# One-time weight sums moved from VectorE to GpSimd, and a ring tile for the fourth difference, in a fused attention and feed-forward kernel

## The chip, the cores and the metric

The kernel runs on one core of a Trainium2 chip. The core has five engines, each with an instruction queue of its own that is worked off in order: TensorE (matrix products; PE in the profile, with PEld for its weight loads), VectorE (DVE), ScalarE (ACT), GpSimd (POOL) and SyncE (SP, which here only issues DMA transfers). GpSimd's queue issues DMA transfers too. Engines wait for one another through semaphores. Data lie in on-chip memory (SBUF), matrix products end in accumulator banks (PSUM), and some intermediate sums are kept in DRAM.

The metric is the time of one execution in device microseconds. The median of three runs before the change is 679.04 us.

## What is computed

Linear attention with a decay for each head, over 4 batches, 8 heads, 768 positions and 64 channels, whose output is the input of a feed-forward block:

```python
for b in range(nb):                     # blocks of 64 positions
    intra = np.einsum('bhic,bhjc->bhij', qb, kb) * Dmask[None]
    intra = np.einsum('bhij,bhjd->bhid', intra, vb)
    inter = np.einsum('bhid,bhde->bhie', qb * lam_pow[None], kv_state)
    out[:, :, sl] = intra + inter
    kb_dec = kb * rev_pow[None]
    kv_state = lam_block[None, :, None, None] * kv_state + np.einsum('bhsd,bhse->bhde', kb_dec, vb)
...
x = attn_out.transpose(0, 2, 1, 3).reshape(B * S, H * D)   # 3072 tokens, 512 channels
h = x @ w_in                                               # 512 x 2048
g = h - np.tanh(h)
return (g @ w_out).astype(np.float32)                      # 2048 x 512
```

All arithmetic is in 32-bit floats.

## The kernel before

The 768 positions are worked in six groups of 128 (`g` is 0 to 5), each with all four batches: 512 tokens. For a group the attention makes `xt`, `up` multiplies with `w_in` in four steps `u`, ScalarE and VectorE apply `h - tanh(h)` and leave the hidden tiles `g11`, `g12`, `g21`, `g22` and `gS1`, and `down` multiplies with `w_out`. From the second group on, a product of two 2x2 block matrices is not made of eight block products but of seven, numbered 1 to 7, by Winograd's form of Strassen's scheme; `FACT` names the two factors of each. The factors are sums and differences of quarters:

- of `w_in` in `sums_in` (L250, four VectorE operations of 128x512 for each `u`: S1, S2, S3 in place, S4),
- of `w_out` in `sums_out` (L256 to L259), kept in DRAM as `factors`,
- of the hidden tiles in `sums_once` (L672) and `seeded_sums`.

Several of the seven products are split by the same scheme once more. Their small factors are made once and serve all later groups:

- `inner_weights(u, ns)` (L531) makes, from the quarters of a factor of `w_in`, four sums of 128x128 (L538) into a tile `ws2` and stores three of them in DRAM as `fine_in` (L539). It is called in the second group (`g` = 1) for factors 2 and 4, then 1, then 5.
- `factors_twice(t)` (L631) does that for a factor of `w_out`: `load_quarters(t)` fetches four quarters from `factors` (L628, tiles `wq` for the first set and `oq` from the pool `opool` after it), then four differences of 128x512 (L636) are made and each is stored in `fine` (L637). `MADE` gives the factor of each of the five sets: 5, 6, 4, 7, 3. The first two sets are made in the second group, one difference in a step; the other three in the third group, two in a step. The table `TURNS` gives the steps.

The tiles `ws2`, `wt1`, `wt2`, `wt4`, the sums `s1` and `s2` of `sums_twice` (L725, L726) and the token sums `tt2` (L548) share one ring of four slots of 128x512, the tag "sums". Whoever takes a slot waits until its former tile is read for good, by a transfer to DRAM too.

`down_twice(g, n, zw)` works a product that is split again: seven groups of four small products (L741), in the order 1, 2, 6, 5, 7, 3, 4. Group 6 needs `s2` (L726), group 3 needs the sum of L746. Its pieces of `fine` come through `piece` (L640), as do those of `factors` and `fine_in`: a ring of eight tiles `wb`, all loaded from GpSimd's queue (L647, L650, L653). Using a piece sends the loads of later ones, up to seven ahead; a load waits until TensorE is done with its slot's former piece. `seeded` does the second product of the hidden layer for `g` from 2 on, `inner_steps` (L566) the products with small factors of `w_in`.

The attention of the group after next is worked between these products (`run(p0[...])`, `run(p1[...])`); in it, `att_state` multiplies keys by their decay on VectorE (L350) before TensorE's kv products (L363).

`hidden(g, c)` is the hidden tile `c` of group `g`. There is one buffer for each `c`, which all groups use in turn. Tile 22 of the third group (`GI` is 2) is first written by the products with factor 5 of `w_in`; in the second group the last to read tile 22 is product 4 of `down`.

Instructions are put in order by a list scheduler at build time; `tc.keep_in_program_order` ties some of them to the program's order.

Of the kernel before, what the change touches and what calls it, by code (L numbers as in the profile page):

```python
# [9 lines left out]
F32 = mybir.dt.float32  # L10
# [6 lines left out]
AL = mybir.AluOpType  # L17
# [7 lines left out]
def kernel(  # L25
# [32 lines left out]
    nc = tc.nc  # L58
# [8 lines left out]
    NU = DFF // 512  # L67
# [55 lines left out]
    raw, late = {}, {}  # L123
# [61 lines left out]
    GI = 2  # L185
# [56 lines left out]
        wt = wst.tile([128, 8, 256], F32, name="wt", tag="w")  # L242
        return wt[:, 0:4], wt[:, 4:8]

    def sums_in(u):
        a11, a12, a21, a22 = (w1[u][:, 2 * c:2 * c + 2, r] for r, c in ((0, 0), (0, 1), (1, 0), (1, 1)))
        s1, s2, s4 = (ws[u][:, x] for x in range(3))
        for dst, x, y, op in ((s1, a21, a22, AL.add), (s2, s1, a11, AL.subtract), (a21, a11, a21, AL.subtract),
                              (s4, a12, s2, AL.subtract)):
            tc.keep_in_program_order(nc.vector.tensor_tensor(dst, x, y, op=op))  # L250

    def sums_out(kt):
        bt, tt = pair[kt]
# [178 lines left out]
    def hidden(g, c):  # L432

        if (g, c) not in hid:
            hid[g, c] = gpool.tile([128, NU, 2, HB], F32, name=f"g{c}", tag=f"g{c}")
        return hid[g, c]
# [85 lines left out]
    def seeded_sums(g, u):  # L522
        g11, g12, g22, s1 = (hidden(g, c)[:, u] for c in (11, 12, 22, "S1"))
        nc.vector.tensor_tensor(s1, g12, g22, op=AL.add)
        nc.vector.tensor_tensor(g12, g11, g12, op=AL.subtract)

    def a_quarter(n, u, i, k):
        wt = {1: w1[u][:, 0:2, 0], 2: w1[u][:, 2:4, 0], 4: w1[u][:, 2:4, 1], 5: ws[u][:, 0]}[n]
        return wt[:, k, ts(i, 128)]

    def inner_weights(u, ns):  # L531
        for n in ns:
            a11, a12, a21, a22 = (a_quarter(n, u, i, k) for i in range(2) for k in range(2))
            t = late["pool"].tile([128, 4, 128], F32, name="ws2", tag="sums", bufs=4)
            s1, s2, s4 = (t[:, x] for x in range(3))
            for dst, x, y, op in ((s1, a21, a22, AL.add), (s2, s1, a11, AL.subtract), (a21, a11, a21, AL.subtract),
                                  (s4, a12, s2, AL.subtract)):
                tc.keep_in_program_order(nc.vector.tensor_tensor(dst, x, y, op=op))  # L538
            nc.gpsimd.dma_start(out=fine_in[INNER.index(n)].rearrange("x p u c -> p u x c")[:, u], in_=t[:, 0:3])  # L539

    def inner_tokens(g, ns):
# [78 lines left out]
    def load_quarters(t):  # L620

        for i in range(2):
            for j in range(2):
                if t == 0:
                    x = late["pool"].tile([128, NU, 128], F32, name="wq", tag="wb", bufs=RING)
                else:
                    x = opool.tile([128, NU, 128], F32, name="oq", tag="o")
                nc.gpsimd.dma_start(out=x, in_=quarter_source(t, i, j))  # L628
                quarters[t, i, j] = x

    def factors_twice(t):  # L631

        b11, b12, b21, b22 = (quarters.pop((t, i, j)) for i in range(2) for j in range(2))
        t1, t2, t4 = (late["pool"].tile([128, NU, 128], F32, name=f"wt{x}", tag="sums", bufs=4) for x in (1, 2, 4))
        for x, dst, a, b in ((5, t1, b12, b11), (6, t2, b22, t1), (7, b12, b22, b12), (4, t4, b21, t2)):
            tc.keep_in_program_order(nc.vector.tensor_tensor(dst, a, b, op=AL.subtract))  # L636
            nc.gpsimd.dma_start(out=fine[TWICE.index(MADE[t]), SUB.index(x)], in_=dst)  # L637
            yield

# [128 lines left out]
    def every(steps):  # L768
        for _ in steps:
            pass  # L770
# [80 lines left out]
    def run(pieces):  # L851
        for fn, *args in pieces:
            fn(*args)
# [38 lines left out]
    for u, c, n, more in turns:  # L892
        every(up_plain(u, (c,)))
        weights(ready["done"] + n)
        run(more)
        if (u, c) == (1, 21):
            load(B + 2)
        if c == 22:
            sums_first(u)
            if u == 1:  # L900
                load_weights(NU * KI)
                load(2 * B)
                powers()
            if u == 2:
                sums_in(0)
# [4 lines left out]
    for kt in range(KH):  # L910
        down_first(kt, (1, 2))
        if kt + 1 < KH:
            sums_out(kt + 1)
        sums_late(kt)
        down_first(kt, (5, 4, 7, 6, 3) if kt + 1 < KH else (5, 6, 7, 4, 3))
        if kt + 3 < KH:
            weights(ready["done"] + 2)
        if kt == 2:
            sums_in(1)
# [4 lines left out]


    TURNS = {1: {t + x: n for n, t in ((0, 7), (1, 14)) for x in range(4)},
             2: {t + x // 2: n for n, t in ((2, 3), (3, 7), (4, 11)) for x in range(4)}}
    making = {}

    def make_factors(g, step):  # L930
        t = TURNS.get(g, {}).get(step)
        if t is not None:
            if t not in making:
                making[t] = factors_twice(t)
            for _ in range(g):
                next(making[t])
            if g == 2 and t < 4 and step in (4, 8):
                load_quarters(t + 1)
# [5 lines left out]
    for g in range(1, NG):  # L944
        last = g == NG - 1
        (p0, p1), step = ahead, 0
        for u in range(NU):
            if g < GI:
                for n in (2, 6, 5, 7, 1, 4, 3):
                    if n != 1:  # L950
                        up(g, u, n)
                    elif u + 1 < NU:
                        up(g, u + 1, 1)
                    else:
                        every(down(g, 1))
                    if u < 2 and n == 5:
                        sums_in(u + 2)
                    step += 1
                    make_factors(g, step)
                inner_weights(u, (2, 4))  # L960
                if u > 1:
                    run(p0[u - 2:u - 1])
                continue
            if u == 0:
                first = down(g, 1)
                if g == 2:
                    load_quarters(2)
            for n in (1, 7) if u == 0 else (6, 3, 1, 7) if u + 1 < NU else (7, 3, 1):
                if n == 1:
                    next(first)  # L970
                else:
                    seeded(g, u + (n == 6), n)
                if n == (7 if u + 1 < NU else 3):
                    seeded_sums(g, u)
                step += 1
                make_factors(g, step)
# [8 lines left out]
        if g < GI:  # L985
            for u in (0, 1):
                inner_weights(u, (1,))
# [4 lines left out]
        if g < GI:  # L992
            for u in (2, 3):
                inner_weights(u, (1,))
# [74 lines left out]
```

## Time and profile before

| what | value |
|---|---|
| median of three runs (lowest, highest) | 679.04 us (677.19, 680.48) |
| the profiled execution | 678.29 us, its span 676.5 us |
| mean granted TensorE clock | 0.992 |
| VectorE busy, share of the span | 490.4 us, 72% |
| GpSimd busy (nearly all of it DMA issues) | 229.2 us, 34% |
| loads of ring pieces from `fine`, L650 | 147, each 540 ns on GpSimd's queue |
| loads of ring pieces from `factors` and `fine_in`, L653 and L647 | 56 and 48 |
| mean rate of DRAM traffic | 201 GB/s |

The profile shows one execution. "Busy" of an engine excludes its waits, and DMA issues of GpSimd count as busy. In the lists of waits a line names the waiting engine, what it would write and its line, then what ended the wait. The table of stretches gives for each stretch of the span its length and the busy time of TensorE, its weight loads, VectorE, ScalarE and GpSimd (instructions in brackets), then the granted clock of TensorE, the DMA engines' busy share and their rate. A timeline line has the start and the length in microseconds, engine, line, operation and tiles, and in square brackets how long the engine had been idle before it and what ended that.

### The profile page before, as it was taken

How to read it: one execution, taken by the hardware profiler on the slowest of the kernel's cores; microseconds unless marked ns; L12 is line 12 of the kernel's file. 1: busy time of each engine (PE TensorE's matmuls, PEld its weight loads, DVE VectorE, ACT ScalarE, POOL GpSimd, SP SyncE). 2: the span in 40 equal slices, each digit the busy share in tenths (PEclk: the TensorE clock that was granted, in tenths of full speed). 3: DMA queues.
4: the chain of work that ended last, by engine and by line, in shares of the span. 5: the costliest groups of instructions: out<-in, count | busy, mean ns of one | idle time of the engine just before them, and what ended most of it. 6: DMA issues, size and time to landing. Idle time of an engine off the chain costs nothing.

```text
span 676.5 us, 13691 instructions
## 1 busy us (share of the span) xinstructions
PE 656.5 (97%) x5112; PEld 601.4 (89%) x5112; DVE 490.4 (72%) x923; ACT 218.4 (32%) x418; POOL 229.2 (34%) x397
## 2 busy tenths in 40 slices
PE   8998999999999899999699999999999999999998
PEld 6787888888888799987599998899998899998897
DVE  4577795737879576677888667998666988557963
ACT  4796825403321112422112233211243211243210
POOL 0001435745422444225444320144420154420261
PEclk9999999999999899999899999999999999999999
DMA  9989888968856778577898876298966176741294
GB/s 212 232 215 268 269 285 248 314 184 229 242 115 154 217 190 252 147 190 232 264 248 233 246 176 128 84 258 232 284 145 139 63 226 207 254 125 48 79 301 152
DMA packets 165475, 136.74 MB, mean 202 GB/s; under 512 B 134688, under 2 KB 135840, under 8 KB 165408
## 3 DMA queue, kind: packets, MB, share of 16 engines
q0 software_dynamic: 31728, 104.36, 48.1%
q1 hardware_dynamic: 133536, 31.50, 23.7%
q8 instruction: 41, 0.67, 0.4%
q14 instruction: 26, 0.21, 0.1%
q10 hardware_dynamic: 144, 0.00, 0.0%
HBM read 109.84 MB, written 25.95 MB: 201 GB/s over the span
## 4 chain that ended last, share of the span: by engine, by line
PE 81%; DMA 6%; DVE 4%; issue 3%; SPq 2%; ACT 1%; POOL 1%; DVEq 0%; POOLq 0%; ACTq 0%
PE y L741 11%; PE zw L741 8%; PE y L566 8%; PE plain L688 8%; PE acc L825 7%; PE y L509 6%; PE h L796 5%; PE y L447 4%; PE z L566 4%; PE zs L509 3%; PE sp L341 3%; PE op L395 2%; PE w L566 2%; DMA raw<-in_moe_w_in_dram 2%; PE z L447 2%
## 5 line engine op out<-in xcount | busy, mean ns | idle before, releaser
L650 POOL DMA_DIRECT2D wb<-fine x147 | 79.2, 540 | 172.0 <-PE plain L688 99.0
L688 PE MATMUL plain<-wb,g 128*128 128x256 f32 x352 | 81.5, 380 | 1.5 <-DVE g L493 1.5
L688 PEld LDWEIGHTS plain<-wb,g 128*128 128x128 f32 x352 | 65.9, 190 | 11.0 <-DVE g L493 2.3
L744 ACT ACTIVATE q<-y 128x128 f32<-128x128 f32 x84 | 23.3, 277 | 142.4 <-PE y L741 140.2
L796 PE MATMUL h<-xt,w 128*128 128x256 f32 x256 | 58.0, 383 | 3.9 <-DVE w L285 3.9
L796 PEld LDWEIGHTS h<-xt,w 128*128 128x128 f32 x256 | 47.7, 190 | 11.7 <-DVE w L285 3.9
L653 POOL DMA_DIRECT2D wb<-factors x56 | 30.2, 541 | 65.0 <-PE y L566 24.0
L741 PE MATMUL y<-wb,g 128*128 128x128 f32 x384 | 51.1, 278 | 0.0
L492 ACT ACTIVATE th<-g 128x512 f32<-128x512 f32 x48 | 29.4, 628 | 63.8 <-DVE g L518 63.8
L570 ACT ACTIVATE g<-y 128x512 f32<-128x512 f32 x48 | 28.5, 593 | 61.1 <-PE y L566 61.1
L741 PEld LDWEIGHTS y<-wb,g 128*128 128x128 f32 x384 | 46.4, 192 | 1.3 <-issue 0.5
L647 POOL DMA_DIRECT2D wb<-fine_in x48 | 25.9, 542 | 41.2 <-PE y L566 17.3
L206 POOL DMA_DIRECT2D raw<-in_moe_w_out_dram x16 | 8.7, 546 | 84.8 <-ACT r L282 59.1
L345 DVE TENSOR_TENSOR ss<-sp,mask 128x512 f32<-128x512 f32 x48 | 30.6, 682 | 9.0 <-PE sp L341 9.0
L741 PE MATMUL zw<-wb,g 128*128 128x128 f32 x256 | 34.8, 279 | 0.0
L493 DVE TENSOR_TENSOR g<-g,th 128x512 f32<-128x512 f32 x48 | 31.6, 685 | 2.7 <-ACT th L492 2.7
L825 PE MATMUL acc<-wt,g 128*128 128x256 f32 x144 | 32.9, 380 | 0.0
L741 PEld LDWEIGHTS zw<-wb,g 128*128 128x128 f32 x256 | 31.8, 195 | 0.1
L825 PEld LDWEIGHTS acc<-wt,g 128*128 128x128 f32 x144 | 27.2, 190 | 4.1 <-DVE g L832 0.4
L509 PE MATMUL zs<-xt,ws 128*128 128x256 f32 x128 | 30.6, 381 | 0.0
L509 PE MATMUL y<-tt,ws 128*128 128x256 f32 x128 | 30.4, 380 | 0.1
L509 PE MATMUL y<-xt,w 128*128 128x256 f32 x128 | 29.7, 379 | 0.0
(214 smaller groups left out, 1483.6 us busy)
## 6 DMA issues: line engine op xcount, KB each, us to landing
wb<-fine POOLq DMA_DIRECT2D x147, 256.0 KB, 4.0
wb<-factors POOLq DMA_DIRECT2D x56, 256.0 KB, 4.1
wb<-fine_in POOLq DMA_DIRECT2D x48, 256.0 KB, 4.2
raw<-in_moe_w_out_dram POOLq DMA_DIRECT2D x16, 512.0 KB, 6.0
v_nat<-in_v_dram SPq DMA_DIRECT2D x24, 256.0 KB, 5.5
fine<-wt POOLq DMA_DIRECT2D x24, 256.0 KB, 4.6
k_nat<-in_k_dram SPq DMA_DIRECT2D x20, 256.0 KB, 4.9
raw<-in_moe_w_in_dram SPq DMA_DIRECT2D x8, 512.0 KB, 6.0
```

Of the source, the lines that this page charges most:

```text
L345: tied(g == 0, nc.vector.tensor_tensor(ss[:, j], sp[j], mask[:, j], op=AL.mult))
L447: nc.tensor.matmul(out=t[:, m, :], lhsT=wt[:, kt, ts(m, 128)], rhs=x[:, kt, :], start=first and m == 0 and kt == 0, stop=kt == 1, skip_gro ...
L492: nc.scalar.activation(th, src, AF.Tanh)
L493: nc.vector.tensor_tensor(dst(c), src, th, op=AL.subtract)
L509: nc.tensor.matmul(out=t[:, m, :], lhsT=wt[:, kt, ts(m, 128)], rhs=x[:, kt, :], start=False, stop=kt == 1, skip_group_check=True)
L566: nc.tensor.matmul(out=dst[:, ts(u, 128)], lhsT=a, rhs=b, start=x in (1, 2, 5) and u == 0, stop=True, skip_group_check=True)
L650: nc.gpsimd.dma_start(out=t.rearrange("p m c -> p (m c)"), in_=fine[TWICE.index(n_), SUB.index(x_)].rearrange("p u c -> p (u c)"))
L653: nc.gpsimd.dma_start(out=t, in_=factors[XAT[FACT[n_][1]]][:, 2 * x_:2 * x_ + 2, :])
L688: nc.tensor.matmul(out=t[:, m, :], lhsT=a[:, u, kt, ts(m, 128)], rhs=wb[:, kt, :], start=first and u == 0 and m == 0 and kt == 0, stop=u = ...
L741: nc.tensor.matmul(out=dst, lhsT=a[:, u, :], rhs=wb[:, ts(u, 128)], start=x in (1, 2) and u == 0, stop=u == NU - 1, skip_group_check=True)
L796: tied(u == 0, nc.tensor.matmul(out=hm[c][:, m, :], lhsT=w1[u][:, i, a, ts(m, 128)], rhs=xt[0, t][:, i, :], start=m == 0 and i == 0, stop= ...
L825: nc.tensor.matmul(out=acc[n][:, r, :], lhsT=a[:, ts(r, 128)], rhs=b, start=kt == 0 and r == 0, stop=kt == KH - 1, skip_group_check=True)
```

## The change

Four edits:

- `sums_in` gets the engine as an argument; for `u` = 2 and 3 its four sums run on GpSimd instead of VectorE.
- `inner_weights` for factors 1 and 5 runs its four sums on GpSimd, and puts them into the buffer of hidden tile 22 of the third group instead of a slot of the ring "sums".
- `factors_twice` no longer writes the third difference over the loaded quarter `b12`, but into a tile `wt3` of its own from the ring. For the fourth and fifth set its differences run on GpSimd.
- In `TURNS` the fifth set starts at step 12 of the third group instead of 11.

```diff
-    def sums_in(u):
+    def sums_in(u, eng=nc.vector):
         a11, a12, a21, a22 = (w1[u][:, 2 * c:2 * c + 2, r] for r, c in ((0, 0), (0, 1), (1, 0), (1, 1)))
         s1, s2, s4 = (ws[u][:, x] for x in range(3))
         for dst, x, y, op in ((s1, a21, a22, AL.add), (s2, s1, a11, AL.subtract), (a21, a11, a21, AL.subtract),
                               (s4, a12, s2, AL.subtract)):
-            tc.keep_in_program_order(nc.vector.tensor_tensor(dst, x, y, op=op))
+            tc.keep_in_program_order(eng.tensor_tensor(dst, x, y, op=op))
...
     def inner_weights(u, ns):
         for n in ns:
             a11, a12, a21, a22 = (a_quarter(n, u, i, k) for i in range(2) for k in range(2))
-            t = late["pool"].tile([128, 4, 128], F32, name="ws2", tag="sums", bufs=4)
+            eng = nc.gpsimd if n in (1, 5) else nc.vector
+            if n in (1, 5):
+                t = hidden(GI, 22)[:, u].rearrange("p m (x c) -> p (m x) c", x=2)
+            else:
+                t = late["pool"].tile([128, 4, 128], F32, name="ws2", tag="sums", bufs=4)
             s1, s2, s4 = (t[:, x] for x in range(3))
             for dst, x, y, op in ((s1, a21, a22, AL.add), (s2, s1, a11, AL.subtract), (a21, a11, a21, AL.subtract),
                                   (s4, a12, s2, AL.subtract)):
-                tc.keep_in_program_order(nc.vector.tensor_tensor(dst, x, y, op=op))
+                tc.keep_in_program_order(eng.tensor_tensor(dst, x, y, op=op))
...
     def factors_twice(t):
 
         b11, b12, b21, b22 = (quarters.pop((t, i, j)) for i in range(2) for j in range(2))
-        t1, t2, t4 = (late["pool"].tile([128, NU, 128], F32, name=f"wt{x}", tag="sums", bufs=4) for x in (1, 2, 4))
-        for x, dst, a, b in ((5, t1, b12, b11), (6, t2, b22, t1), (7, b12, b22, b12), (4, t4, b21, t2)):
-            tc.keep_in_program_order(nc.vector.tensor_tensor(dst, a, b, op=AL.subtract))
+        t1, t2, t3, t4 = (late["pool"].tile([128, NU, 128], F32, name=f"wt{x}", tag="sums", bufs=4)
+                          for x in (1, 2, 3, 4))
+        eng = nc.gpsimd if t > 2 else nc.vector
+        for x, dst, a, b in ((5, t1, b12, b11), (6, t2, b22, t1), (7, t3, b22, b12), (4, t4, b21, t2)):
+            tc.keep_in_program_order(eng.tensor_tensor(dst, a, b, op=AL.subtract))
             nc.gpsimd.dma_start(out=fine[TWICE.index(MADE[t]), SUB.index(x)], in_=dst)
             yield
...
-             2: {t + x // 2: n for n, t in ((2, 3), (3, 7), (4, 11)) for x in range(4)}}
+             2: {t + x // 2: n for n, t in ((2, 3), (3, 7), (4, 12)) for x in range(4)}}
...
-                        sums_in(u + 2)
+                        sums_in(u + 2, nc.gpsimd)
```

## Prediction

> **What bounds the kernel now.** I read the page first, then TensorE's waits, then stretches of the span with the granted clock, then the order of work around the two longest waits. The page's first part says that TensorE is the bound, with 20 us of its span not busy:
>
> ```profile
> span 676.5 us, 13691 instructions
> PE 656.5 (97%) x5112; PEld 601.4 (89%) x5112; DVE 490.4 (72%) x923; ACT 218.4 (32%) x418; POOL 229.2 (34%) x397
> ```
>
> TensorE's waits, asked for between 145 and 345 us, leave only three kinds there (columns: total, times, longest); every other one of more than a moment lies before 99 us, which the change does not touch:
>
> ```profile
> PE kv L363 <- DVE k_nat L350: 4.9, 1, 4.9
> PE zw L741 <- DVE gS L746: 3.0, 1, 3.0
> PE plain L688 <- DVE g L493: 1.5, 2, 1.1
> ```
>
> In the stretches around these (the column after the busy times is the granted clock), TensorE runs at 0.74 of its clock for 6.6 us behind the 3.0 us wait, and at 0.53 for 6.5 us behind the 4.9 us wait. That costs 6.6 x 0.26 = 1.7 us and 6.5 x 0.47 = 3.1 us more.
>
> ```profile
> 227.40:230.40 3.00, 0.00 (x0) 0.00 (x0) 1.29 (x2) 0.28 (x1) 1.26 (x3) 1.00 0.93 276
> 230.40:237.00 6.60, 6.59 (x57) 6.25 (x58) 2.71 (x6) 0.28 (x1) 1.08 (x2) 0.74 0.90 260
> 329.70:334.70 5.00, 0.09 (x3) 0.04 (x2) 5.00 (x10) 0.28 (x1) 2.57 (x5) 0.93 0.80 293
> 334.70:341.20 6.50, 6.50 (x55) 6.38 (x56) 6.01 (x10) 0.28 (x1) 1.08 (x2) 0.53 0.80 177
> ```
>
> So all that the change could win is **place one**, 227 us: 3.0 + 1.7 = 4.7 us, and **place two**, 321 to 341 us: 1.5 + 4.9 + 3.1 = 9.5 us. VectorE's timeline tells what ended each. At place one VectorE waits to overwrite slots of the ring "sums" that the transfers of L539 still read; at place two it waits for nothing, it is late:
>
> ```profile
> 225.56 0.69 DVE L725 TENSOR_TENSOR s<-g 128x512 f32<-128x512 f32 x1 [2.32 <-DMA fine_in<-ws]
> 229.06 0.69 DVE L726 TENSOR_TENSOR s<-s,g 128x512 f32<-128x512 f32 x1 [2.08 <-DMA fine_in<-ws]
> 229.67 0.68 DVE L746 TENSOR_TENSOR gS<-gS,s 128x512 f32<-128x512 f32 x1
> ...
> 314.96 0.69 DVE L636 TENSOR_TENSOR wt<-oq 128x512 f32<-128x512 f32 x1 [4.16 <-DMA oq<-factors]
> ...
> 333.93 1.28 DVE L350 TENSOR_TENSOR k_nat<-k_nat,mask 128x512 f32<-128x512 f32 x2
> ```
>
> **What the moved work costs on GpSimd.** 48 instructions leave VectorE: 8 of L250 and 8 of L636 (128x512), 32 of L538 (128x128). Back to back VectorE starts them 0.60 and 0.20 us apart (timeline), so it is freed of 16 x 0.60 + 32 x 0.20 = 16 us. GpSimd runs no two-input operation before. The nearest rows:
>
> ```profile
> L636 DVE TENSOR_TENSOR wt<-oq,wt 128x512 f32<-128x512 f32 x8 | 5.5, 687 | 1.1 <-DVE g L493 0.9 <-DMA fine<-wt 0.2
> L538 DVE TENSOR_TENSOR ws<-w,ws 128x128 f32<-128x128 f32 x12 | 3.4, 281 | 0.0
> masks.py:199 POOL TENSOR_SCALAR_AFFINE_SELECT ident<-ident 128x128 f32<-128x128 f32 x1 | 0.3, 287 | 0.1
> ```
>
> Lower ends: VectorE's own 0.68 and 0.28 us. Upper ends: GpSimd's one-input row, four times for 512 elements and twice for the second input, 8 x 0.287 = 2.30 us, and 0.57 us. I take 1.5 and 0.4 us, nearer to GpSimd's own row (4 x 0.287 = 1.15) than to its double.
>
> The Trainium skill (GPSIMD Engine Reference, section "Performance versus the Vector engine") times a two-input fp32 sum at 1.96 times VectorE's; by that 0.687 becomes 1.35 us, and the sum below would come out about 1 us lower.
>
> TensorE's own instructions stay the same; in the built program it only makes five groups of products in another order, at places one and two. The fifth set's turn comes one step (1.7 us) later: its four differences and four stores are used from 369 us on, so only the slots that they hold count, below.
>
> **First part, 147 to 199 us: L250 and the fourth tile.** TensorE waits for nothing here. In the built program L250 stands on GpSimd's queue behind the quarter loads (156 us) and behind the third store of the first set (about 170 us). TensorE needs the results at 174.8 and 187 us, so 4 x 1.5 = 6 us each time are hidden. Past them the queue moves ring loads that TensorE uses from 192 us on. The new wait is another: L636's third difference no longer overwrites a loaded quarter but takes the ring's next slot, and so waits until the store of the first difference has landed, with L468 right behind it on VectorE; TensorE's next z products wait for L468. First set: that store lands 2.8 us after 166.41, the third difference runs at 169.2, L468 ends by 170.6, needed at 171.4: nothing lost. Second set: GpSimd gets there by 172.9 + 3 x 1.5 + 3 loads x 0.54 = 179.0 instead of 178.73, the store lands 2.8 us later, L468 ends at 183.2, needed at 183.5. Cost 0, with 0.3 us of cover; at 2.30 us a sum, 4 x 0.8 - 0.3 = 2.9 us.
>
> **Place one.** L538 for factors 1 and 5 writes into the unused hidden tile. By the built program L725 and L726 then wait only for older L539 transfers, issued at 209.12 and 210.53, that have landed long before; L746 runs at about 225 us, needed at 227.1. The 4.7 us go. On GpSimd eight sums (8 x 0.4) and two stores (2 x 0.76) now stand between the loads of the next product's pieces. Those were issued in one burst once the L539 stores let them, and now start each time a product ends:
>
> ```profile
> 222.84 0.76 POOL L539 DMA_DIRECT2D fine_in<-ws  x1 [4.25 <-DVE ws L538]
> 224.93 3.73 POOL L650 DMA_DIRECT2D wb<-fine  x7
> ```
>
> The fifth of them now starts at about 229.6 us, lands some 4.5 us later (median of this line 4.0; behind the burst more) and is needed at 234.7: 0.6 us of cover. At 0.57 us a sum it loses 0.5 to 1 us. Factor 5's sums end by about 256 us; their pieces are needed at 267: hidden.
>
> **Place two.** VectorE loses the eight L636 of the fourth and fifth set (4.8 us) and the 4.16 us wait for their loads. It then reaches L350 at about 324 us, needed at 328, so both waits named above (1.5 and 4.9 us) go. What is late next: the built program lets L725 and L726 of the next product (x 6) wait until the stores of the fifth set's first and second difference have landed, as these hold the ring's slots. GpSimd's chain to there, from the landing of the fourth set's loads at 314.9: four sums, a load and three stores, 4 x 1.5 + 0.75 + 3 x 0.55 = 8.4, so 323.3; the fifth set's load lands 4.4 us on (median of the loads at 317 to 324 us), 327.7; a sum, a ring load, a store, two sums: 3 x 1.5 + 1.1 = 5.6, so 333.3; the store lands 3.7 us on (median at 326 to 333 us), 337.0; L726 0.6: 337.6 us. TensorE is there at 329.7 and waits 7.9 us, where it waited 6.4. VectorE's queue stood still meanwhile; with the half clock again (three groups at 1.6 us, as before) and one more wait of 1.0 us for the next L746, twelve VectorE operations behind, TensorE ends the following sp products at 353.3, before at 352.6: **0.7 us lost**, 9.5 us of waiting turned into some 10.
>
> **Sum.** 4.7 - 0.7 - 0 = 4.0 us gained. The profiled execution took 678.29 us (span 676.5); 674.3 by that, and since it lies 0.75 us under the median of 679.04, **675 us** against the median.
>
> Ends: with 0.68 us a sum L726 is done at 331.9, TensorE waits 2.2, 2.1 and 1.0 us with no half clock and gains 5 us at place two: 4.7 + 5.0, so 669.3. With 2.30 us L726 is done at 343.2: 6.3 lost at place two, 2.9 in the first part, 0.5 at place one: 4.7 - 9.7, so 684.1.
>
> **Rivals.**
> *GpSimd's sums get through only when VectorE is not summing.* For it: VectorE is busy 12.8 of the 15.7 us from 314 to 329.7, where the fourth set falls. Against it: it has 4.8 us less to do, and the fifth set falls where it waits. The fourth set would start at about 324 instead of 314.9: 9.1 us later in the chain, 9.1 + 0.7 - 4.7 = 5 us lost, **684 us**. It decides once the seven sums of the chain take 4.0 / 7 = 0.6 us more each, 2.1 us.
> The Trainium skill (SBUF — State Buffer, section "Who interferes with whom") speaks for this: a VectorE operation with two inputs in SBUF and a GpSimd operation that reads SBUF exclude each other for their whole length. No run here shows it yet.
> *GpSimd nearly as fast as VectorE*: **669 us**, worked out above. Against it: 287 ns for one input of 128 elements.
> *Place one's wait only moves*: the pieces behind GpSimd's sums land late. For it: 0.6 us of cover, and these loads took over 5 us in the old burst. Then TensorE waits 2 to 3 us at 233 us and slows again: 4.7 given back, **679 us**.
>
> **How the numbers follow.** The forecast has 0.40, the slow rival 0.25, the moved wait 0.20, the fast one 0.15. A measurement of this kernel can tell about 0.5% (3.4 us) from no change: faster is below 675.6, slower above 682.4. The forecast lies at the edge (0.26 faster, 0.12 same, 0.02 slower), the fast rival is faster, the moved wait 0.17 same and 0.03 slower, the slow one 0.02 same and 0.23 slower: 0.41, 0.31, 0.28. The range reaches to both ends of the sum's price, 669 to 684; for faster alone it is 669 to 675.
>
> **What would show it.** Right: no wait of TensorE near 227 us and full clock to 320; L725 or L726 waiting for a store of L636 near 330, TensorE's longest wait there, behind L726 instead of L350; a GpSimd row of 128x512 near 1.5 us. Wrong: TensorE waiting for z products at 183 us (first part mis-sized), for a ring load at 233 us, or GpSimd sums of 2 us and more beside a busy VectorE.

## The result, and the profile after

The changed kernel takes 684.91 us (median of 8 runs, 682.61 to 687.53), the kernel before, measured beside it, 678.17 us (8 runs). The ratio is 1.0099, 95% interval 1.007 to 1.0127: the change makes the kernel 1% slower, where 675 us and a gain of 4 us were forecast. The profiled execution took 686.18 us. Its first lines:

```profile
span 684.4 us, 13692 instructions
PE 658.2 (96%) x5112; PEld 603.2 (88%) x5112; DVE 490.7 (72%) x875; ACT 218.3 (32%) x418; POOL 265.8 (39%) x445
```

VectorE has 48 instructions fewer (875 against 923) and is busy as long as before (490.7 against 490.4 us). By the prediction's step widths the 48 were worth 16 us, so others must have become longer. That is the first thing to look for. TensorE's waits (total, times, longest) show two of the three old places changed and new ones beside them:

```profile
PE y L747 <- issue: 3.8, 1, 3.8
PE kv L363 <- DVE k_nat L350: 2.9, 1, 2.9
PE z L447 <- DVE g L468: 2.8, 1, 2.8
PE zw L747 <- DVE g L752: 1.9, 1, 1.9
PE zw L747 <- DMA wb<-fine: 1.1, 1, 1.1
```

The 3.0 us wait for L752 (L746 before) at 227 us is gone. The wait before z L447 is new: the sign that the prediction named for a mis-sized first part. "issue" in the first line means that the profile found no releaser; the timeline below shows one.

To see where the time went, TensorE's instructions of the two traces are set side by side, and the shift of each against the same instruction of before is read off. Where the shift changes, time is lost or won. The changed kernel was profiled a second time later (span 681.5 us):

| stretch (us of before) | predicted | first profile | second profile |
|---|---|---|---|
| up to 183, before any difference on TensorE's path | 0 | +2.1 | +0.1 |
| z L447 at 183.7 and the half clock behind it | 0 | +4.6 | +6.3 |
| place one, 227 to 236 | -4.7 | -4.9 | -4.9 |
| ring pieces, 239 to 256 | 0 | +2.7 | +2.6 |
| place two, 319 to 357 | +0.7 | +3.4 | +0.8 |
| sum | -4.0 | +7.9 | +5.0 |

The sums are those of the values before rounding. The first row is no part of the change: it comes from loads and conversions in the first 75 us, which both kernels have alike, and in the other kernels below it lies between -0.3 and +4.4 us.

**The first part.** GpSimd's and VectorE's timelines of the changed kernel (start, length, engine, line; in brackets the idle time before it and what ended it):

```profile
177.92 1.28 POOL L250 TENSOR_TENSOR w<-w 128x512 f32<-128x512 f32 x1
179.15 1.27 POOL L250 TENSOR_TENSOR ws<-w,ws 128x512 f32<-128x512 f32 x1
183.81 0.55 POOL L643 DMA_DIRECT2D fine<-wt  x1 [1.82 <-DVE ws L542]
```

```profile
178.35 2.64 DVE L456 TENSOR_TENSOR g<-g,th 128x512 f32<-128x512 f32 x1 [0.76 <-ACT th L455]
187.32 0.69 DVE L642 TENSOR_TENSOR wt<-oq 128x512 f32<-128x512 f32 x1 [1.47 <-DMA fine<-wt]
187.93 0.68 DVE L468 TENSOR_TENSOR g<-g,z 128x512 f32<-128x512 f32 x1
```

The same L456 before the change, and the one of the changed kernel 18 us earlier, which meets three of GpSimd's sums (below):

```profile
175.22 0.69 DVE L456 TENSOR_TENSOR g<-g,th 128x512 f32<-128x512 f32 x1 [0.76 <-ACT th L455]
```

```profile
160.36 3.91 DVE L456 TENSOR_TENSOR g<-g,th 128x512 f32<-128x512 f32 x1 [0.70 <-ACT th L455]
```

L456 at 178.35 waits for nothing that the profile names, and takes 2.64 us instead of 0.69. It ends at 180.99, 0.57 us after GpSimd's second sum (179.15 + 1.27 = 180.42). Its operands are both in SBUF. The L456 and L473 at 176.31 and 176.91, which read PSUM, ran beside a GpSimd sum (from 176.69) at 0.68 us. The 1.95 us pass on to the first difference of the second set, its store goes out at 183.81, and the third difference waits 1.47 us for it to land, with L468 behind it. TensorE then stops and comes back at 0.55 of its clock (column after the busy times):

```profile
185.60:188.76 3.16, 0.34 (x3) 0.03 (x1) 1.69 (x5) 0.11 (x1) 1.71 (x3) 0.94 0.86 270
188.76:192.10 3.34, 3.34 (x9) 2.72 (x10) 1.84 (x3) 1.52 (x3) 0.66 (x2) 0.55 0.64 191
```

**Place one.** L731 and L732 (L725 and L726 before) now run at once, and L752 is done 1.8 us before TensorE needs it at 233.84; the clock is 1.00 from 223 to 237 us:

```profile
227.59 0.68 DVE L731 TENSOR_TENSOR s<-g 128x512 f32<-128x512 f32 x1
228.30 0.69 DVE L732 TENSOR_TENSOR s<-s,g 128x512 f32<-128x512 f32 x1
231.36 0.71 DVE L752 TENSOR_TENSOR gS<-gS,s 128x512 f32<-128x512 f32 x1 [1.18 <-PE zw L747]
```

Ten microseconds later a ring piece is late, the sixth of the next product. GpSimd issued its load at 238.28, behind eight sums and two stores, and it landed at 243.61:

```profile
243.75 1.13 PE L747 MATMUL zw<-wb,g 128*128 128x128 f32 x8 [1.10 <-DMA wb<-fine]
```

**Place two.** From 319 to 333 us, VectorE sums with two SBUF inputs take 1.7 to 2.2 us where they meet GpSimd's (L524, L525, L678; two of L493 3.10 us together), so L350 comes at 333.01 and TensorE still waits 2.9 us for it. Then s1 and s2 wait for stores of the fifth set. TensorE's 3.8 us before y ("issue" above) end 0.1 us behind L732:

```profile
326.03 2.23 DVE L678 TENSOR_TENSOR g<-gS,g 128x512 f32<-128x512 f32 x1
333.01 1.28 DVE L350 TENSOR_TENSOR k_nat<-k_nat,mask 128x512 f32<-128x512 f32 x2
338.04 1.64 DVE L731 TENSOR_TENSOR s<-g 128x512 f32<-128x512 f32 x1 [3.15 <-DMA fine<-wt]
341.62 0.69 DVE L732 TENSOR_TENSOR s<-s,g 128x512 f32<-128x512 f32 x1 [1.35 <-DMA fine<-wt]
```

And the price of the sums on GpSimd, from the groups (busy, mean ns of one):

```profile
L642 POOL TENSOR_TENSOR wt<-oq 128x512 f32<-128x512 f32 x4 | 5.1, 1283 | 5.3 <-DMA oq<-factors 5.3
L542 POOL TENSOR_TENSOR g<-ws 128x128 f32<-128x128 f32 x4 | 2.9, 722 | 0.1
L542 POOL TENSOR_TENSOR g<-g,w 128x128 f32<-128x128 f32 x4 | 1.9, 466 | 0.1
```

1.28 us for 128x512, under the 1.5 that was taken; 0.47 us for 128x128 when undisturbed and 0.72 on average for the group that meets VectorE's sums most, over the 0.4 that was taken.

### The profile page after: what moved, and what is told of

The parts are those of the page before. It is cut to its first block, busy times and chain, and to the rows that moved or that the text cites. A ratio compares the mean times of both kernels' runs of the same rounds, so it can differ in the third digit from the quotient of the medians.

```text
span 684.4 us, 13692 instructions
## 1 busy us (share of the span) xinstructions
PE 658.2 (96%) x5112; PEld 603.2 (88%) x5112; DVE 490.7 (72%) x875; ACT 218.3 (32%) x418; POOL 265.8 (39%) x445
## 4 chain that ended last, share of the span: by engine, by line
PE 71%; DMA 11%; POOL 7%; issue 4%; SPq 3%; DVE 2%; ACT 2%; DVEq 0%; POOLq 0%; ACTq 0%
PE y L747 10%; PE plain L694 9%; PE y L570 8%; PE zw L747 8%; PE y L509 7%; PE h L802 6%; PE z L570 4%; PE zs L509 3%; PE sp L341 3%; PE op L395 2%; PE w L570 2%; DMA raw<-in_moe_w_in_dram 2%; DMA oq<-factors 2%; DMA fine<-wt 2%; PE acc L831 2%
## 5 line engine op out<-in xcount | busy, mean ns | idle before, releaser
L747 PE MATMUL y<-wb,g 128*128 128x128 f32 x384 | 52.8, 284 | 0.0
L747 PEld LDWEIGHTS y<-wb,g 128*128 128x128 f32 x384 | 48.0, 197 | 1.3 <-issue 0.3
L493 DVE TENSOR_TENSOR g<-g,th 128x512 f32<-128x512 f32 x48 | 33.4, 724 | 2.9 <-ACT th L492 2.9
L578 DVE TENSOR_TENSOR g<-r,y 128x512 f32<-128x512 f32 x16 | 11.0, 688 | 26.6 <-PE y L570 26.6
```

What stands on the lines that cost most here:

```text
L493: nc.vector.tensor_tensor(dst(c), src, th, op=AL.subtract)
L747: nc.tensor.matmul(out=dst, lhsT=a[:, u, :], rhs=wb[:, ts(u, 128)], start=x in (1, 2) and u == 0, stop=u == NU - 1, skip_group_check=True)
```

## The experiments

All ratios are to the kernel before, run beside it on the same chip.

| kernel | w_in sums (L250) | factors 1, 5 | fourth tile | sets 4, 5 | turn | ratio | interval |
|---|---|---|---|---|---|---|---|
| changed | GpSimd | GpSimd, hidden | yes | GpSimd | 12 | 1.0099 | 1.007 to 1.0127 |
| u1_win_vec | VectorE | GpSimd, hidden | yes | GpSimd | 12 | 1.0016 | 0.9995 to 1.0038 |
| u2_sets_vec | GpSimd | GpSimd, hidden | yes | VectorE | 12 | 1.0065 | 1.0039 to 1.0092 |
| u3_only_inner | VectorE | GpSimd, hidden | no | VectorE | 11 | 1.001 | 0.999 to 1.003 |
| u4_tile_vec | VectorE | VectorE, hidden | no | VectorE | 11 | 0.9959 | 0.9936 to 0.9983 |
| u5_only_t3 | VectorE | VectorE, ring | yes | VectorE | 11 | 1.0002 | 0.9972 to 1.0031 |
| u6_only_win | GpSimd | VectorE, ring | no | VectorE | 11 | 1.0047 | 1.0021 to 1.0073 |
| u7_tile_turn | VectorE | VectorE, hidden | no | VectorE | 12 | 0.9926 | 0.99 to 0.9952 |
| u8_all_vec | VectorE | VectorE, hidden | yes | VectorE | 12 | 0.9945 | 0.9924 to 0.9966 |
| u11_sets_gp | VectorE | VectorE, hidden | no | GpSimd | 12 | 0.9993 | 0.9967 to 1.0019 |

**The w_in sums: undone in the changed kernel, and alone.**

```
u1_win_vec, against the changed kernel
-                        sums_in(u + 2, nc.gpsimd)
+                        sums_in(u + 2)
u6_only_win, against the kernel before
-    def sums_in(u):
+    def sums_in(u, eng=nc.vector):
...
-            tc.keep_in_program_order(nc.vector.tensor_tensor(dst, x, y, op=op))
+            tc.keep_in_program_order(eng.tensor_tensor(dst, x, y, op=op))
...
-                        sums_in(u + 2)
+                        sums_in(u + 2, nc.gpsimd)
```

> The changed kernel with one part undone: the four sums of L250 of the third and fourth group of w_in are made on VectorE again. Theory A (the sums exclude each other): a VectorE sum with both inputs in SBUF can't run beside a GpSimd sum and waits for a whole run of them; at 178 us L456 took 2.64 us for that, and the late L468 behind it stopped TensorE for 3.0 us with 1.6 us of half clock after. So without them the wait before z L447 near 186 us shrinks to 0.5 us at most, there is no half-clock window there, and the kernel is 4 us faster than the changed one: ratio to before about 1.004. Theory B (the ring's slots): the stop comes from the fourth tile, which lets the third difference wait for a store; then the wait before z L447 stays above 2 us and the ratio stays near 1.010.

> The kernel before with only the sums of L250 of the third and fourth group of w_in on GpSimd: no fourth tile, all else as before. Theory A (exclusion): VectorE's L456 at 178 us waits for a run of GpSimd's sums as in the changed kernel, L468 comes late and z L447 waits some 3 us with half clock behind: ratio 1.006 to 1.009. Theory B (it takes the fourth tile's wait for a store as well): z L447 waits 1 us at most, ratio 1.003 or below.

Undone: 1.0016 instead of 1.0099, so these eight sums cost 0.0083, 5.6 us, somewhat more than the 4 us expected. In its trace the shift at z L447 does not change by 0.2 us. But u1 differs in one thing more. In its order VectorE runs L468 ahead of the second set's third difference (181.93 and 182.53), as in u5 and u8 below, and in the changed kernel behind it. So u1 alone does not rule out theory B, the fourth tile's wait for a store.

Alone: 1.0047, 3.2 us. L456 takes 3.92 us at 162.58 and 2.22 at 179.56, the fourth difference waits 1.42 us for the store of the first, with L468 behind it, z L447 waits 1.9 us, and 3.8 us are lost between 183 and 188 us. That is below what was expected of theory A and above B. The stop comes without the fourth tile, so theory B falls as the whole cause.

The changed kernel's 4.6 and 6.3 us have more in them. Its L642 waits 0.40 and 1.63 us for slots at 172 and 175 us, and VectorE reaches the L456 of 178 us some 1.1 us later than before, measured against TensorE; in u6 it does not. In u1, u5 and u8 VectorE is as late there without a loss, but L468 stands ahead of the wait. (The fourth tile serves the third difference of each set, not the fourth as the title has it.)

The w_in sums do one thing more on GpSimd's queue: three ring loads now go out behind them and just ahead of the store of the second set's first difference (180.36 to 181.99, the store at 183.81), and are still under way with it. In the five traces with these sums on GpSimd this store takes 3.5 to 5.9 us to land, in the eight others 2.3 to 3.2. That the loads are the reason is not shown by itself.

**The factor sets.** u2 puts them back on VectorE in the changed kernel; u11 puts them on GpSimd in the best kernel, with the third difference in place.

```
u2_sets_vec, against the changed kernel
-        eng = nc.gpsimd if t > 2 else nc.vector
+        eng = nc.vector
u11_sets_gp, against u7_tile_turn
+            eng = nc.gpsimd if t > 2 else nc.vector
-            tc.keep_in_program_order(nc.vector.tensor_tensor(dst, a, b, op=AL.subtract))
+            tc.keep_in_program_order(eng.tensor_tensor(dst, a, b, op=AL.subtract))
```

> The changed kernel with another part undone: the fourth and fifth set of factor differences (L642) on VectorE again, still with the fourth tile and one step later. Theory A: the five VectorE sums between 319 and 333 us that took 1.7 to 2.2 us instead of 0.68 go back to 0.69, L350 comes some 4 us sooner, TensorE has no wait behind L731 and L732, and the 3.4 us that the stretch from 325 to 360 us lost against before come back: ratio about 1.005. Theory B (the fifth set is simply one step late and holds the slots): L731 and L732 still wait for its stores, TensorE still waits 2 us or more behind them, and at most 1.5 us come back: ratio 1.008 or more.

> The kernel before with the hidden tile on VectorE and the fifth set one step later (0.9926 by itself), and the fourth and fifth set on GpSimd, with the third difference in place. Theory A (the sums of these sets exclude VectorE's): between 315 and 330 us five of VectorE's two-input sums take 1.7 us or more, L350 comes late, and 3.4 us of the gain are lost: ratio 0.9977. Theory B (in the changed kernel the fourth tile's slots made the loss): L731 and L730 wait less than 1 us for stores, and no more than 1.5 us are lost: ratio 0.995 or below.

u2: 1.0065; its stretch from 325 to 357 us gains 1.75 us against before, no VectorE sum there is long, and TensorE waits for nothing behind L731 and L732. But L350 does not come 4 us sooner, as theory A had it: with the sets' sums before it on VectorE again it starts at 338.23, 332.3 without the shift of 5.9 us, where the changed kernel has 328.5, and kv waits 3.4 us. So what costs at place two is less the late L350 than the wait for the stores. u11: 0.9993 against 0.9926, 4.5 us for the sets on GpSimd, with wide intervals; place two in the two traces shows 2.1 us of it. But neither theory had its course right: with VectorE otherwise on time, L350 is nearly on time too (kv waits 2.1 us), and the loss is TensorE's 4.4 us before y. It stands behind s2, which waits 3.83 us for a store of the fifth set. So the fourth tile isn't needed for that wait. The same stands in u1_win_vec, whose VectorE and TensorE show it bare:

```profile
331.89 1.55 DVE L731 TENSOR_TENSOR s<-g 128x512 f32<-128x512 f32 x1 [4.84 <-DMA fine<-wt]
```

```profile
PE y L747 <- issue: 5.6, 1, 5.6
```

**Factors 1 and 5: the engine or the tile.** Both kernels make them in the hidden tile; u3 on GpSimd, u4 on VectorE.

```
u4_tile_vec, against the kernel before (u3_only_inner: eng = nc.gpsimd if n in (1, 5) else nc.vector)
-            t = late["pool"].tile([128, 4, 128], F32, name="ws2", tag="sums", bufs=4)
+            eng = nc.vector
+            if n in (1, 5):
+                t = hidden(GI, 22)[:, u].rearrange("p m (x c) -> p (m x) c", x=2)
+            else:
+                t = late["pool"].tile([128, 4, 128], F32, name="ws2", tag="sums", bufs=4)
...
-                tc.keep_in_program_order(nc.vector.tensor_tensor(dst, x, y, op=op))
+                tc.keep_in_program_order(eng.tensor_tensor(dst, x, y, op=op))
```

> The kernel before with one part of the change: the sums of L538 for factors 1 and 5 on GpSimd, into the hidden tile. Both theories: TensorE's wait near 227 us and the half clock behind it go (4.9 us in the changed kernel), and about 2.5 us come back as ring loads that are late at 241 and 255 us behind GpSimd's sums: ratio 0.9965, between 0.994 and 0.999. If this part brings nothing by itself, the ratio is 1.000 or above.

> The kernel before with only the place of these sums changed: factors 1 and 5 into the hidden tile, still on VectorE. Theory A: what ended the wait near 227 us was the slot, not the engine, so the 4.9 us come all the same, and with the ring loads not behind GpSimd's sums nothing comes back: ratio 0.993. Rival (the gain needed VectorE to be freed): less than the kernel with the sums on GpSimd gains, ratio 0.998 or above.

In both traces place one wins 4.9 us. In u4 none of it is lost again by 256 us, 0.7 us is at place two, and the ratio is 0.9959, a smaller gain than the 0.993 expected. In u3 2.9 us are lost again before 256 us (two pieces late by 0.8 us each, a wait of 0.7 us before plain, and what follows), and the ratio is 1.001, above the expected range: this part brings nothing by itself. The tile was worth all of the gain, and GpSimd took it away: 0.0051, 3.4 us.

**The fourth tile, the later turn, everything on VectorE.**

```
u5_only_t3, against the kernel before
-        t1, t2, t4 = (late["pool"].tile([128, NU, 128], F32, name=f"wt{x}", tag="sums", bufs=4) for x in (1, 2, 4))
+        t1, t2, t3, t4 = (late["pool"].tile([128, NU, 128], F32, name=f"wt{x}", tag="sums", bufs=4)
+                          for x in (1, 2, 3, 4))
...
-        for x, dst, a, b in ((5, t1, b12, b11), (6, t2, b22, t1), (7, b12, b22, b12), (4, t4, b21, t2)):
+        for x, dst, a, b in ((5, t1, b12, b11), (6, t2, b22, t1), (7, t3, b22, b12), (4, t4, b21, t2)):
...
u7_tile_turn, against u4_tile_vec
-             2: {t + x // 2: n for n, t in ((2, 3), (3, 7), (4, 11)) for x in range(4)}}
+             2: {t + x // 2: n for n, t in ((2, 3), (3, 7), (4, 12)) for x in range(4)}}
u8_all_vec, against the changed kernel
-            eng = nc.gpsimd if n in (1, 5) else nc.vector
+            eng = nc.vector
...
-        eng = nc.gpsimd if t > 2 else nc.vector
+        eng = nc.vector
...
-                        sums_in(u + 2, nc.gpsimd)
+                        sums_in(u + 2)
```

> The kernel before with one part of the change, the fourth tile: the third difference of each set takes a slot of the ring, on VectorE. Theory A: its wait for a store lies beside other work where VectorE is on time, so the time stays: ratio 1.000, between 0.998 and 1.002. Theory B (the slots are what costs): z L447 waits near 183 us and L725 or L726 wait for stores near 330 us, ratio 1.004 or above.

> The kernel before with the hidden tile for factors 1 and 5, on VectorE, and the fifth set one step later, but with the third difference in place, without the fourth tile. If the 1.75 us of the stretch from 325 to 357 us come from the later turn: ratio 0.993. If the fourth tile brings them: 0.996, as with the hidden tile alone.

> The changed kernel with all its sums on VectorE: the hidden tile, the fourth tile and the later turn of the fifth set stay, nothing runs on GpSimd. If each part stands by itself (theory A), the hidden tile brings its 4.9 us near 227 us, and the stretch from 325 to 357 us gains 1.75 us as it did with the sets on VectorE: ratio 0.993 (0.991 to 0.996). If the parts need each other (VectorE too full with all sums and the fourth tile's waits), z L447 near 183 us waits again and the ratio is 0.997 or above.

u5: 1.0002, no new wait of TensorE. u7: 0.9926, and in its trace the stretch from 325 to 357 us gains 1.3 us against before. u8: 0.9945, within the interval of u7, so no price of the fourth tile on VectorE can be told. **u7_tile_turn beats both kernels**: 672.58 us where the kernel before took 677.4. It keeps the change's hidden tile and its later turn, and none of the sums on GpSimd.

**Do the sums exclude each other?** The first of four kernels that compute nothing of the reference:

> Nothing of the reference is computed; seven stages set VectorE sums of 128x512 (0.60 us apart when alone) against GpSimd work, each engine's instructions back to back: 16 VectorE sums alone, 8 GpSimd sums alone, both, VectorE with one input in PSUM beside GpSimd sums, VectorE beside one-input GpSimd copies, VectorE beside GpSimd memsets, and 32 VectorE sums of 128x128 beside GpSimd sums. Theory A (exclusion of two-input sums): the third stage takes the sum of the two alone, 16 x 0.60 + 8 x 1.23 = 19.4 us, the fourth only the longer, 9.8 us. Rival (they share a way in and slow each other a little, or not at all): the third takes 10 to 12 us. For the copies theory A says the sum again, for the memsets only the longer of the two.

VectorE's runs of 128x512 in it, in the order of the expectation (columns as above; the second stage has none):

```profile
11.37 11.59 DVE L76 TENSOR_TENSOR g<-a,b 128x512 f32<-128x512 f32 x16 [5.33 <-DMA g<-in_q_dram]
40.69 20.06 DVE L76 TENSOR_TENSOR g<-a,b 128x512 f32<-128x512 f32 x16
63.53 11.51 DVE L80 TENSOR_TENSOR g<-a,p 128x512 f32<-128x512 f32 x16
78.55 14.83 DVE L76 TENSOR_TENSOR g<-a,b 128x512 f32<-128x512 f32 x16
96.28 12.53 DVE L76 TENSOR_TENSOR g<-a,b 128x512 f32<-128x512 f32 x16
```

Alone 11.59 us; beside GpSimd sums 20.06; with one input in PSUM 11.51, nothing lost. The last, beside memsets, loses 12.53 - 11.59 = 0.94 us, which is put down to the one GpSimd sum that joins the stages and runs into each of the later ones (here from 96.32). So a GpSimd sum costs VectorE (20.06 - 11.59 - 0.94) / 8 = 0.94 us, a copy (14.83 - 11.59 - 0.94) / 8 = 0.29, a memset nothing. Theory A stands for the sums, whose third stage it put at 19.4 us; for the copies it was too dear by far. GpSimd's eight sums took 13.26 us there and 10.64 alone: both engines pay.

The Trainium skill (SBUF — State Buffer, section "Who interferes with whom") states just this: a VectorE instruction with two SBUF inputs contends with a GpSimd instruction that reads SBUF, not with one that only writes, and one with at most one SBUF input, outside what the page calls 2-port modes, does not. These stages agree, with the numbers above.

**Runs of sums, or turns?** In the changed kernel another L456 took even 3.91 us, from 160.36, beside three GpSimd sums in a row (159.99, 161.22 and 162.44 to 163.70).

> Nothing of the reference is computed; stages as in the first kernel of pairs, but every sum writes a tile of its own turn, so that each engine's instructions really follow one another: 16 VectorE sums of 128x512 alone, 8 GpSimd sums alone, both, both with a memset of 128x128 behind each GpSimd sum, VectorE beside 8 GpSimd copies, then 32 VectorE sums of 128x128 alone, 16 GpSimd sums of 128x128 alone, and both. Theory A1 (a run of GpSimd sums keeps VectorE out until it ends, as at 160 us, where L456 took 3.91 us): in the third stage one VectorE sum takes some 9 us and the stage 9.6 + 9.8 = 19.4 us. Theory A2 (the two take turns, one sum each): the stage takes about the same, but no VectorE sum takes more than 2 us. With memsets between, both theories say turns. Copies: some 0.3 us each lost to VectorE, as the first kernel showed. Sums of 128x128: VectorE loses the length of GpSimd's, 0.41 us each.

> Nothing of the reference is computed; stages: 10 VectorE sums that come singly, each behind a ScalarE copy of its own result, alone; the same beside a run of 8 GpSimd sums; 8 GpSimd sums in the shape and order of L250 (slices of a weight tile, each needing one before) alone; 16 VectorE sums one after the other beside these; the single VectorE sums beside these. Theory S (a sum that comes singly, with none queued behind it, stays out until GpSimd's run ends): in the second and fifth stage one VectorE sum takes 6 us or more. Theory W (L250's slices are what keeps VectorE out): the second stage shows turns, no VectorE sum above 2 us, the fourth and fifth one of 4 us or more. Neither: turns in all of them.

> Nothing of the reference is computed; three stages with the same work, 10 single VectorE sums beside 8 GpSimd sums in L250's shape: alone with each other, then with 16 matmuls of 128x512 running on TensorE meanwhile, then with these and twelve transfers of 256 KB. If busy TensorE or transfers are what let a run of GpSimd's sums keep VectorE out in the changed kernel, one VectorE sum of the second or third stage takes 3 us or more. If not, all take 1.0 to 1.8 us and the engines take turns in all three, and the cause of the 3.9 us stays open.

m2: VectorE's 16 sums take 17.18 us beside GpSimd's eight, which start 1.67 us apart instead of 1.22: turns, and 17.18 us again with the memsets between. GpSimd's first sum was over before VectorE began; each of the other seven made one VectorE sum 1.74 to 1.76 us long instead of 0.68, a cost of 1.07 us, a little above m1, where VectorE's sums start 0.72 us apart and not 0.60. Copies make one 0.98 to 1.09 us long, a cost of 0.3 to 0.4. For 128x128 VectorE's 32 take 9.92 instead of 6.55 us; thirteen of them meet a GpSimd sum and take 0.54 us instead of 0.28, 0.26 us each, less than the 0.41 expected. m3 and m4: turns in every stage, no VectorE sum that stands singly above 1.74 us, with single sums, with L250's slices, with 32 matmul passes running and with twelve transfers. None of the four makes a run that holds VectorE out; A1, S, W and the guess at TensorE and the transfers all fall.

In the kernel itself it is otherwise:

```
u9_gap, against the changed kernel
+    scratch = const.tile([128, 128], F32, name="scratch")
...
             tc.keep_in_program_order(eng.tensor_tensor(dst, x, y, op=op))
+            if eng is nc.gpsimd:
+                tc.keep_in_program_order(nc.gpsimd.memset(scratch, 0.0))
```

> The changed kernel with a GpSimd memset of a 128x128 scratch tile behind each of L250's sums on GpSimd; the memset reads nothing. Theory A1 (a run of GpSimd sums keeps VectorE out until it ends): in the gap VectorE gets in, the L456 of 160 and 178 us take at most 2 us (before 3.91 and 2.64), z L447 waits 1.5 us less and the kernel is 1 to 3 us faster than the changed one, ratio 1.006 to 1.008. Theory A2 (what decides is only how many sums there are): nothing changes, ratio 1.010.

```profile
162.07 1.05 DVE L460 TENSOR_TENSOR g<-g,th 128x512 f32<-128x512 f32 x1 [0.69 <-ACT th L459]
191.47 0.69 DVE L646 TENSOR_TENSOR wt<-oq 128x512 f32<-128x512 f32 x1 [3.86 <-DMA fine<-wt]
```

The first line is the 3.91 us sum of the changed kernel: 1.05 us, and the one of 178 us takes 1.11 (two others, at 176 and 178 us here, 2.21 and 1.75). The gaps let VectorE in, as A1 said. The time is not what it said: 1.0147 (1.0112 to 1.0183), slower still. Against TensorE's own progress the first difference's store goes out 0.6 us sooner than in the changed kernel's first profile, but it takes 5.88 us to land, instead of 3.49. The three ring loads before it take 5.2 to 6.6 us instead of 3.6 to 4.4; why they do is open. The third difference waits 3.86 us for the store and z L447 4.6 us. So the same stop has two doors: the sums that keep VectorE out, and the landing of the store that the third difference waits for. This does not explain the slower time: behind the start the shifts of u9 add up to 6.0 us, those of the changed kernel to 5.8 and 5.0 in its two profiles. Its start is 3.8 us late, which is no part of the change; why its median is higher stays open.

**The changed kernel once more.**

> The changed kernel once more, for a second profile of it: the start up to 125 us (2.1 us later than before in the first one) is no part of the change and should fall anywhere between 0 and 4 us, the wait before z L447 near 186 us should be 2.5 to 3.5 us again, and the stretch from 325 to 357 us should lose 1 to 3.5 us; in the kernels with GpSimd sets and one part undone it lost 0.8 to 1.4 us. Ratio 1.007 to 1.013.

1.0109 (1.0079 to 1.0139). Its profile is in the table of the result: start +0.1, first part +6.3 (z L447 waits 4.4 us, beyond the expected range), place two +0.8, just below the expected range. L456 takes 3.94 and 2.63 us again; the first difference's store takes 4.50 us to land.

## Why the prediction was wrong, point by point

**The first part: the step that failed.** "Cost 0, with 0.3 us of cover" counted when GpSimd gets to the store of the second set's first difference, and took VectorE to be on time for it. VectorE was not: GpSimd's own sums had kept it out for 1.95 us at 178 us, and the slots had held it up by some 1.1 us before that (1.6 in the second profile). So the store went out at 181.7 (182.3 in the second profile), without the shift of the start, instead of 179.0. A second term was mis-sized: the store, with three ring loads just ahead of it, took 3.49 and 4.50 us to land, where 2.8 was counted. Together that is 3.4 and 5.0 us against 0.3 us of cover: a stop, of 2.8 and 4.4 us, with 1.6 to 1.8 us lost at the lower clock behind it. It cost 4.6 and 6.3 us in the two profiles, and u1's ratio puts GpSimd's w_in sums at 5.6 us. Nothing else in the forecast was off by as much. The exclusion was among the rivals, but priced at place two only, as GpSimd's sums being late. It was VectorE that waited, in the stretch that was written off as hidden.

**Place one: right, to 0.2 us.** 4.7 forecast, 4.9 measured in both profiles, by the mechanism named: the slots. u4 shows that the engine had no part in it.

**The cover of 0.6 us behind it: too small.** The rival "place one's wait only moves" came true in a weaker form: 2.6 us given back, by pieces 0.3 to 1.1 us late, a wait of 1.0 us before plain and the clock behind them, instead of 4.7. The eight sums took 4.7 us on the queue (0.46 to 0.92 each, the long ones beside VectorE's) instead of 3.2. The fifth piece, which the forecast looked at, went out those 1.5 us later but landed in 3.7 us, in time; the sixth, right behind it, took 5.3 us and was late. So two terms were mis-sized: the price of a 128x128 sum, 0.4 us, and the landing of the pieces, put at 4.5 us for each.

**Place two: the mechanism right, the size uncertain.** s1 and s2 did wait for the fifth set's stores, and L732 was done at 342.3 us; 337.6 plus the shift of 4.5 us that TensorE brought along is 342.1. That agreement is partly luck: sums of 1.28 us made the chain shorter than 1.5 us would, and a load of the fifth set that GpSimd awaited for 3.0 us made it longer. L350 was forecast at "about 324 us" and came at 328.5 and 328.3 in the two profiles, without the shifts, since VectorE's sums were stretched, by some 6.5 and 6.3 us in all. With 0.8 us lost in the second profile, and 1.3, 1.4 and 0.8 us in u1, u9 and u11, the 0.7 us of the forecast is near. The 3.4 us of the first profile are the exception, and not for longer sums: the last two loads of its fifth set went out 1.4 us later against TensorE's progress and took 6.8 us to land instead of 5.1, so that L732 was done 1.9 us later, and the clock was at 0.50 to 0.58 in three stretches (336 to 338.5, 342.4 to 346 and 349 to 352 us), in the second profile in one (340 to 346). Why the loads took longer is open. Against the same turn on VectorE (1.2 to 1.75 us gained in u8, u7 and u2) the sets on GpSimd are a loss in each case.

**GpSimd's price.** 1.28 us for 128x512 lies under the 1.5 taken; 1.28 / 0.687 is 1.86 times VectorE's. The Trainium skill (GPSIMD Engine Reference, section "Performance versus the Vector engine") has 1.96, near enough. The faster price did not help: what counted was what the sums do to VectorE and to the transfers behind them on GpSimd's queue, not how long one of them takes.

**The sum.** With the measured terms, 5.6 (w_in, u1) - 4.9 + 2.7 (place one and the pieces) + 0.8 (place two) = 4.2 us slower, against 6.7 us between the medians (4.8 to 8.6 by the interval); the first profile's larger place two would fill the gap. The range went up to 684, for GpSimd sums of 2.30 us or for the slow rival at place two. It left out that the same exclusion strikes in the first part as well. That the rival's 684 us lies close to the measured 684.91 is luck: it had the fourth set start at 324 us instead of 314.9, and the set started at 319.00, which is 314.5 without the shift.

What stays open: why in the kernel a run of GpSimd's w_in sums without gaps kept VectorE out (3.91, 3.92, 3.92 and 3.94 us in four profiles), while runs of the same sums took turns with it in every kernel of sums alone. That a gap lifts it is shown; its cause is not.

## What to carry to other kernels

Before moving work to GpSimd to free VectorE, look at which VectorE instructions run in the same stretch: those with two SBUF inputs lose about what GpSimd's sums take, and a "hidden" sum is hidden only if VectorE's neighbours are not on a short path to TensorE. Ask of each such move which part of it is the buffer and which the engine; here the buffer (a free tile, a later turn) was worth 0.7%, and the engine cost more than that. And an engine that issues the loads of a ring is a poor place for extra work: each sum there stands in front of a transfer.

## What the runs showed of the hardware

- A two-input GpSimd sum of 128x512 takes 1.28 us and costs a busy VectorE 0.94 us (m1) or 1.07 us (m2) if that reads two SBUF operands, nothing if one is in PSUM. One of 128x128 takes 0.47 us and costs 0.26. A GpSimd copy of 128x512 costs 0.3 to 0.4 us, a memset nothing.
- In this kernel a VectorE sum waited out three GpSimd sums in a row; a memset of 0.2 us between them let it in.
- Behind stops of 1.9, 2.8, 3.0, 4.4 and 4.6 us at z L447 TensorE lost another 1.8, 1.6, 3.0, 1.8 and 1.8 us, which the length of the stop does not order; where the clock was read, it was 0.55 for 3.3 us (behind the stop of 2.8 us).
- The start of the kernel, the same in all of these, differs by some 5 us between single executions, so two profiles are compared stretch by stretch and not by their spans.
